# State copies for two units at once, weight sums rounded two slots later, and a reordered start in a scan and feed-forward kernel

## The chip, the cores and the metric

The kernel runs on one core of a Trainium2 chip. The metric is the device time of one execution in microseconds (us). The engines are TensorE (PE, with its weight loads shown as PEld), VectorE (DVE), ScalarE (ACT), GpSimd (POOL) and SyncE (SP), which issues nearly all transfers. Each engine works through its own queue in the order of the program and waits where an operand is not there yet.

## The reference

A chunked linear attention, followed by a two-layer feed-forward block over all its tokens:

```python
# x (4, 8, 768, 32), a (4, 8, 768), B and C (4, 8, 768, 16), chunks of 32
cum = np.cumsum(log_a_of_chunk, axis=-1)
M = einsum(Cc, Bc) * exp(cum_i - cum_j) * causal
y = M @ xc + (Cc @ state) * exp(cum)
state = exp(sum(la)) * state + sum_j(Bc_j * xc_j * exp(cum_last - cum_j))
...
h = y_tokens @ w_in                 # 3072 x 256 by 256 x 2048
out = np.maximum(0.01 * h, h) @ w_out   # 2048 x 256
```

## The kernel before

All engines' queues are written out by hand: an instruction stands in its engine's queue where the Python code issues it, and the framework only adds the waits.

**The scan.** The sequence is cut into 8 chunks of 96 steps, times 4 batches: 32 units `u`, unit `u` being batch `b = u % 4` of chunk `c = u // 4`. A unit covers all 8 heads. For each unit the loop issues `scores(u + 1)` (products of C and B on PE, L387, multiplied by the decay matrix `lt` on DVE, L394), `outputs(u)` (products with the inputs and the state, L405, then copies out of PSUM by ACT), `states(u)` inside it (products for the next chunk's state, L436), and `decay(u + 3)` (a product of `dl` and `dr`, L365, with an exponential on ACT, L358, which gives `lt`). The states leave PSUM by one ACT copy into `stage` (L442), and four POOL copies (L447), one for each of four heads' places, put them into rows 96 to 111 of the next chunk's input tile `xss[c + 1]`, where the unit four later reads them. `state_decay(c + 1)`, once a chunk behind the unit with `b == 1`, multiplies the next B tile `bn` by its decays on POOL (L375); PE's state products of the next chunk need it. Loads for the chunk after the next are issued by SP at `b == 2` and `b == 3`, the `bn` tile last.

**The start.** Units 0 and 1 get their decays by another way (`decay_direct`, L351, from `reach` tiles made on POOL); `fill_less` on DVE and one copy on ACT fill rows of `dr` for the later units; L472 and L473 make `erev`, the decays for `bn`. `keep_warm` (L202) multiplies zeros so that PE has something to do. The surplus load: `fetch_w(0)` is called twice, and the first tile it loads is never read.

**The weights** come as 64-bit numbers and are decoded on the way: five passes for each of 16 blocks `f`, on DVE with help by ACT. From unit 10 on one pass follows each unit (`decode(1)`), 22 in all; in the feed-forward part three passes follow each group.

**The feed-forward part.** Matrices are split into a high and a low part, a product is three PE instructions (L556). The first two token blocks are done for 16 weight blocks in 32 groups: six products of the first layer into one of four PSUM banks, `activate` on ACT (L542, L543), the low half on DVE (L547), which frees the bank, and from the fifth group on six products of the second layer. The other four token blocks use fused products (`strassen`), which need sums of weight blocks (`sh`, `sl`) and of tokens (`token_forms`, which start in `decoded()` when all passes are done). A weight sum is five or four operations on POOL (L129, L139), a rounding to `sh` on ACT (L148, in `sums_high`) and the rest `sl` on POOL (L149). For the first two pairs of blocks, decoded during the scan, the sums are rebuilt ahead of the feed-forward loop (`rebuilt_sums`).

Of the kernel before, what the change touches and what calls it, by code (L numbers as in the profile page):

```python
# [47 lines left out]
def scan_ffn(ctx: ExitStack, tc: tile.TileContext, a_l, bc_l, c_l, bn_l, x_l, w_l, out_l):  # L48
# [75 lines left out]
        add_weights(q, w32s[f - 1][:, :2 * 128], w32s[f][:, :2 * 128])  # L124

    def rebuilt_sums(q):
        a = spare[2].rearrange("p (n c) -> p n c", n=2)
        f = slice(2 * q, 2 * q + 2)
        nc.gpsimd.tensor_tensor(  # L129
            out=a, in0=wh[:, f, :2 * 128], in1=wl[:, f, :2 * 128], op=ALU.add  # L130
        )
        add_weights(q, a[:, 0], a[:, 1])
        settle(2 * q + 1)

    def add_weights(q, a1, a2):
        s = s32s[q] = spare[q % 2].rearrange("p (n c) -> p n c", n=4)

        def tt(out, in0, in1, op):
            nc.gpsimd.tensor_tensor(out=out, in0=in0, in1=in1, op=op)  # L139

        tt(s[:, 0], a2[:, :128], a2[:, 128:], ALU.add)
        tt(s[:, 1], s[:, 0], a1[:, :128], ALU.subtract)
        tt(s[:, 2], a1[:, :128], a2[:, :128], ALU.subtract)
        tt(s[:, 3], a1[:, 128:], s[:, 1], ALU.subtract)
        defer(sums_high, 2 * q + 1)

    def sums_high(f):
        nc.scalar.copy(sh[:, f // 2], s32s[f // 2])  # L148
# [1 line left out]
            out=sl[:, f // 2], in0=s32s[f // 2], in1=sh[:, f // 2], op=ALU.subtract  # L150
        )

    spare, owed = None, collections.deque()
    ready = set()

    def decode_rest(f):
# [78 lines left out]
        alloc_x(c)  # L235
    fetch_x(0)
    fetch_bn(0)
    fetch_w(0)

    upto = sc1.tile([Q, QE], F32, name="upto")  # L240
    upto_b = sc1.tile([Q, QE], BF16, name="upto_b")
# [156 lines left out]
    def outputs(u):  # L398
        c, b = divmod(u, NB)
        kk = QE if c else Q  # L400
        mt, xs = lts[u], xss[c][:, b]
        bank = 6 + u % 2
        for h in range(NH):
            g, hh = divmod(h, 4)
            nc.tensor.matmul(  # L405
                ps[hh * D:(hh + 1) * D, bank, g * Q:(g + 1) * Q],
                lhsT=xs[:kk, h * D:(h + 1) * D], rhs=mt[:kk, h, :], start=True, stop=True,
            )
        if u:
            states(u)  # L410
        yp = ps[:, bank, :2 * Q].rearrange("p (g i) -> p g i", g=2)
        i = 0
        while i < Q:
            t, col = divmod(u * Q + i, TS)
            n = min(Q - i, TS - col)
            to, of = slice(col, col + n), slice(i, i + n)
            if t < 2:
                hi = xfa[:, 2 * t:2 * t + 2, 0, to]
                nc.scalar.copy(hi, yp[:, :, of])
                nc.vector.tensor_tensor(  # L420
                    out=xfa[:, 2 * t:2 * t + 2, 1, to], in0=yp[:, :, of], in1=hi, op=ALU.subtract
                )
            else:
                nc.scalar.copy(y[:, t - 2, :, to], yp[:, :, of])
            i += n

    def states(u):
# [4 lines left out]
        if c + 1 < NC:  # L432
            for h in range(NH):
                g, hh = divmod(h, 4)
                n0 = (b * NH + h) * N
                nc.tensor.matmul(  # L436
                    ps[hh * D:(hh + 1) * D, bank, 2 * Q + g * D:2 * Q + (g + 1) * D],
                    lhsT=bns[c][:kk, n0:n0 + 2 * N], rhs=xs[:kk, h * D:(h + 1) * D],
                    start=True, stop=True,
                )  # L440
            stage = pst.tile([128, 2, D], F32, name="stage")
            nc.scalar.copy(  # L442
                stage, ps[:, bank, 2 * Q:2 * Q + 2 * D].rearrange("p (g d) -> p g d", g=2)
            )
            to = xss[c + 1][Q:QE, b].rearrange("n (g h d) -> n g h d", g=2, d=D)
            for hh in range(4):
                nc.gpsimd.tensor_copy(to[:, :, hh], stage[hh * D:hh * D + N])  # L447

    nc.vector.tensor_scalar(
        out=la, in0=la, scalar1=1e-6, scalar2=1.0, op0=ALU.max, op1=ALU.min,  # L450
# [5 lines left out]
    nc.scalar.activation(la[:, DIRECT * NH:], la[:, DIRECT * NH:], AF.Ln)  # L456
    nc.vector.tensor_copy(after_r, after)
    nc.vector.tensor_copy(dl[:Q], upto_b.unsqueeze(1).to_broadcast([Q, SLOTS, QE]))
    nc.scalar.copy(
        dr[Q:Q + 3 * NH, 0], less[Q:Q + 3 * NH].unsqueeze(2).to_broadcast([3 * NH, NH, Q])  # L460
    )
    for u in range(DIRECT):
        fill_reach(u)
    decay_mask(DEC)
    decay_mask(6)
    split_sums(0, 0, nc.scalar)
    fill_less(1)
    decay_direct(0, DEC)
    decay_exp(0, DEC)
    scores(0)  # L470
    fill_less(2)
    nc.tensor.matmul(ps[:QE, DEC, :ncols], lhsT=after, rhs=la, start=True, stop=True)  # L472
    nc.scalar.activation(erev, ps[:QE, DEC, :ncols], AF.Exp)  # L473
    decay_direct(1, 6)
    fetch_rows(DIRECT, 4)
    decay_exp(1, 6)
    state_decay(0)
    fetch_bc(1)
    fetch_x(1)
# [4 lines left out]
    for u in range(NU):  # L484
# [1 line left out]
        if u + 1 < NU:  # L486
            scores(u + 1)
        outputs(u)
        if u == 1:
            states(0)  # L490
        if u == 0:
            keep_warm(DEC, 4)
            decay(2)
# [10 lines left out]
        if u == 4:  # L504
            split_sums(1, 7)
        if u == 0:
            fill_less(3)
        if 1 <= u <= 4:
            fill_later(u + 3, u + 4)
# [14 lines left out]
    tmp = late.tile([128, 6, TS], F32, name="tmp")  # L524
    ob = late.tile([128, 4, TS], F32, name="ob")
    c1, u2, u3 = (tmp[:, i] for i in range(3))
    spare = [tmp[:, i] for i in range(3)]

    jobs = collections.deque()

# [76 lines left out]


    def decoded():
        settle()  # L610
        dec.close()
        xfb = ctx.enter_context(
            tc.tile_pool(name="xfb", bufs=1, side="right", reuse_waits="tile")
# [4 lines left out]
        for js in token_forms(1):  # L618
            jobs.extend(js)

    for q in owed:
        rebuilt_sums(q)
    behind = 4
    for q in range(NP):
        for e in range(2):
            f = 2 * q + e
            assert f in ready
            for t in range(2):
                bank = 2 * e + t
                for k in range(2):  # L630
                    x = xfa[:, 2 * t + k]
                    product(ps[:, bank], layer_one(f, k), (x[:, 0], x[:, 1]), k == 0, k == 1)
                low = activate(bank, f, t)
                if passes:
                    decode(3)
                    settle()
                    if not passes:
                        decoded()
                low()
                work(2)  # L640
                if q or len(todo) > behind:
# [104 lines left out]
```

## Time and profile before

| | before |
|---|---|
| median of 3 runs | 348.39 us (347.0 to 351.26) |
| the profiled execution, its own time | 344.38 us |
| its span in the profile | 342.7 us |
| mean granted PE clock | 0.97 |
| scan, from the start to the first product of the feed-forward part | 79.25 us |
| feed-forward part, to the end | 263.4 us |

A row of a timeline reads: start, duration, engine, line, operation, out<-in, count, and in brackets the idle time of the engine before it with what ended it. Rows that are merged show the whole stretch with its count. In a window of time the columns are the busy time of PE, PEld, DVE, ACT and POOL with the instructions in brackets, then the granted clock, the share of DMA time and GB/s. In a group the columns are count, busy time, mean ns of one, and the idle time before it. PE rows that overlap are pipelined; their ends are modelled.

### The profile page before, as it was taken

How to read it: one execution, taken by the hardware profiler on the slowest of the kernel's cores; microseconds unless marked ns; L12 is line 12 of the kernel's file. 1: busy time of each engine (PE TensorE's matmuls, PEld its weight loads, DVE VectorE, ACT ScalarE, POOL GpSimd, SP SyncE). 2: the span in 40 equal slices, each digit the busy share in tenths (PEclk: the TensorE clock that was granted, in tenths of full speed). 3: DMA queues.
4: the chain of work that ended last, by engine and by line, in shares of the span. 5: the costliest groups of instructions: out<-in, count | busy, mean ns of one | idle time of the engine just before them, and what ended most of it. 6: DMA issues, size and time to landing. Idle time of an engine off the chain costs nothing.

```text
span 342.7 us, 6283 instructions
## 1 busy us (share of the span) xinstructions
PE 320.9 (94%) x2406; PEld 249.8 (73%) x2407; DVE 214.3 (63%) x367; ACT 187.4 (55%) x369; POOL 116.7 (34%) x202
## 2 busy tenths in 40 slices
PE   6899979799499999999999989999999999999995
PEld 3465646456388888888888868888888888888884
DVE  7398858575599999332376536665547666545661
ACT  4356848561776776565365446554466455445451
POOL 8175688888454454884000053000040000000000
PEclk9699989879899999999999999999999999999999
DMA  7745963903033330000002000000003000000003
GB/s 222 206 147 135 260 192 114 264 5 122 2 130 122 118 124 0 0 2 0 0 28 98 0 0 2 0 0 0 2 0 122 2 0 2 2 0 0 0 2 122
DMA packets 10273, 21.83 MB, mean 64 GB/s; under 512 B 2723, under 2 KB 4611, under 8 KB 10243
## 3 DMA queue, kind: packets, MB, share of 16 engines
q1 hardware_dynamic: 10099, 21.35, 20.1%
q8 instruction: 19, 0.31, 0.4%
q14 instruction: 11, 0.09, 0.1%
q10 hardware_dynamic: 144, 0.07, 0.1%
HBM read 18.13 MB, written 3.29 MB: 63 GB/s over the span
## 4 chain that ended last, share of the span: by engine, by line
PE 74%; issue 12%; POOL 10%; ACT 2%; DVE 2%; POOLq 0%; ACTq 0%; DVEq 0%
PE ps L556 61%; PE ps L387 4%; POOL xs L447 4%; PE ps L365 3%; PE ps L405 3%; POOL tmp L139 1%; POOL bn L375 1%; PE ps L436 1%; POOL tmp L129 1%; ACT lt L358 1%; DVE lt L394 1%; POOL xfa L296 1%; PE ps L202 1%; PE ps L351 1%; POOL xfa L591 0%
## 5 line engine op out<-in xcount | busy, mean ns | idle before, releaser
L556 PE MATMUL ps<-gs,wh 128*128 128x512 f32 x384 | 135.8, 389 | 0.0
L542 ACT ACTIVATE gs<-ps 128x512 fp32r<-128x512 f32 x96 | 57.4, 598 | 68.5 <-DVE ps L658 36.6
L547 DVE TENSOR_TENSOR gs<-ps,gs 128x512 fp32r<-128x512 f32 x96 | 65.8, 685 | 31.1 <-ACT ps L543 31.0
L556 PEld LDWEIGHTS ps<-gs,wh 128*128 128x128 f32 x384 | 72.2, 188 | 15.1
L556 PE MATMUL ps<-gs,wl 128*128 128x512 f32 x192 | 74.7, 389 | 0.0
L556 PE MATMUL ps<-xfa,wh 128*128 128x512 f32 x160 | 57.7, 397 | 5.7 <-DVE gs L547 5.7
L543 ACT ACTIVATE ps<-ps 128x512 f32<-128x512 f32 x96 | 56.9, 593 | 0.0
L658 DVE TENSOR_TENSOR tmp<-ps,tmp 128x512 f32<-128x512 f32 x32 | 22.1, 691 | 54.5 <-PE ps L556 49.3
L394 DVE TENSOR_TENSOR lt<-ps,lt 112x384 f32<-112x384 f32 x64 | 32.7, 552 | 19.0 <-PE ps L387 17.7
L447 POOL COPY xs<-stage 16x64 f32<-16x64 f32 x112 | 38.4, 343 | 16.6 <-ACT stage L442 10.8
L556 PEld LDWEIGHTS ps<-gs,wl 128*128 128x128 f32 x192 | 36.1, 188 | 7.5
L556 PEld LDWEIGHTS ps<-xfa,wh 128*128 128x128 f32 x160 | 30.6, 191 | 12.6 <-DVE gs L547 6.2
L556 PE MATMUL ps<-xfb,sh 128*128 128x512 f32 x96 | 36.0, 389 | 0.0
L658 DVE TENSOR_TENSOR ps<-ps,tmp 128x512 f32<-128x512 f32 x48 | 33.6, 699 | 2.5
L556 PE MATMUL ps<-xfa,wl 128*128 128x512 f32 x80 | 31.6, 395 | 0.0
L358 ACT ACTIVATE lt<-ps 112x768 f32<-112x768 f32 x32 | 26.0, 812 | 7.8 <-PE ps L351 3.5
L556 PE MATMUL ps<-xfb,wh 128*128 128x512 f32 x64 | 25.0, 391 | 1.5 <-ACT tmp L661 1.5
L387 PE MATMUL ps<-bc 32*112 32x192 f32 x256 | 24.8, 407 | 1.4 <-DVE lt L394 1.3
L387 PEld LDWEIGHTS ps<-bc 32*112 32x112 f32 x256 | 12.8, 189 | 12.3 <-DVE lt L394 6.8
L591 POOL TENSOR_TENSOR xfb<-tmp,xfb 128x512 fp32r<-128x512 f32 x6 | 7.7, 1293 | 40.2 <-ACT xfb L595 40.2
L556 PEld LDWEIGHTS ps<-xfb,sh 128*128 128x128 f32 x96 | 18.0, 188 | 3.8
L661 ACT COPY tmp<-ps 128x512 f32<-128x512 f32 x16 | 9.4, 587 | 18.4 <-PE ps L556 18.4
(93 smaller groups left out, 390.0 us busy)
## 6 DMA issues: line engine op xcount, KB each, us to landing
raw<-w_l SPq DMA_DIRECT2D x17, 512.0 KB, 4.2
xs<-x_l SPq DMA_DIRECT2D x8, 384.0 KB, 4.7
out_l<-ob SPq DMA_DIRECT2D x12, 256.0 KB, 2.1
bn<-bn_l SPq DMA_DIRECT2D x8, 231.0 KB, 6.2
bc<-bc_l SPq DMA_DIRECT2D x6, 224.0 KB, 3.6
bc<-bc_l SPq DMA_DIRECT2D x2, 608.0 KB
bc<-c_l SPq DMA_DIRECT2D x12, 96.0 KB, 3.2
dr<-parts_d SPq DMA_DIRECT2D x11, 9.0 KB
```

What stands on the lines that cost most here:

```text
L358: nc.scalar.activation(lt.rearrange("p (g h) i -> p g (h i)", g=2), ps[:QE, bank:bank + 2, :4 * Q], AF.Exp)
L365: nc.tensor.matmul(ps[:QE, DEC + g, :4 * Q].rearrange("p (h i) -> p h i", i=Q), lhsT=dl[:KD, b], rhs=dr[:KD, b, 4 * g:4 * g + 4], start=Tr ...
L387: nc.tensor.matmul(ps[:QE, r, :2 * Q].rearrange("p (h i) -> p h i", h=2), lhsT=bc[rows, b * QE:(b + 1) * QE], rhs=spread[rows, :, b], star ...
L394: nc.vector.tensor_tensor(out=lt[:, g], in0=ps[:QE, g, :2 * Q], in1=lt[:, g], op=ALU.mult)
L405: nc.tensor.matmul(ps[hh * D:(hh + 1) * D, bank, g * Q:(g + 1) * Q], lhsT=xs[:kk, h * D:(h + 1) * D], rhs=mt[:kk, h, :], start=True, stop= ...
L447: nc.gpsimd.tensor_copy(to[:, :, hh], stage[hh * D:hh * D + N])
L542: nc.scalar.activation(g[:, 0], hp, AF.Prelu, alpha=0.01)
L543: nc.scalar.activation(hp, hp, AF.Prelu, alpha=0.01)
L547: nc.vector.tensor_tensor(out=g[:, 1], in0=hp, in1=g[:, 0], op=ALU.subtract)
L556: nc.tensor.matmul(out, lhsT=w[a], rhs=x[b], start=start and i == 0, stop=stop and i == 2, skip_group_check=more,)
L658: nc.vector.tensor_tensor(out=out, in0=ps[:, bank], in1=u, op=ALU.add)
L661: nc.scalar.copy(c1, ps[:, 0])
```

## The change

Four edits. The state copies: `states` of an even unit only issues its products; that of the odd unit copies both units' states with one ACT copy and four POOL copies of twice the size. The surplus load goes. The weight sums: `sums_high` is put on a list and runs two groups later; the two rebuilt sums are issued in the loop, with scratch tiles of their own, and `decoded()` waits for the list to be empty. The start: the row fills for slot 1 move to ACT, those for slot 2 behind unit 0; two warming products are added; unit 1's decay products come ahead of L472.

```diff
     def rebuilt_sums(q):
-        a = spare[2].rearrange("p (n c) -> p n c", n=2)
+        a = spare[4 + q % 2].rearrange("p (n c) -> p n c", n=2)
...
-        settle(2 * q + 1)
     def add_weights(q, a1, a2):
-        s = s32s[q] = spare[q % 2].rearrange("p (n c) -> p n c", n=4)
+        s = s32s[q] = spare[q % 4].rearrange("p (n c) -> p n c", n=4)
...
-        defer(sums_high, 2 * q + 1)
+        delayed.append([2, sums_high, 2 * q + 1])
...
+    def late_sums():
+        for d in list(delayed):
+            d[0] -= 1
+            if d[0] < 0:
+                delayed.remove(d)
+                d[1](d[2])
...
     fetch_bn(0)
-    fetch_w(0)
...
+        if u == 1:
+            states(0)
         if u:
             states(u)
...
-            stage = pst.tile([128, 2, D], F32, name="stage")
+            if b % 2 == 0:
+                return
+            stage = pst.tile([128, 2, 2, D], F32, name="stage")
             nc.scalar.copy(
-                stage, ps[:, bank, 2 * Q:2 * Q + 2 * D].rearrange("p (g d) -> p g d", g=2)
+                stage, ps[:, 6:8, 2 * Q:2 * Q + 2 * D].rearrange("p b (g d) -> p b g d", g=2)
             )
-            to = xss[c + 1][Q:QE, b].rearrange("n (g h d) -> n g h d", g=2, d=D)
+            to = xss[c + 1][Q:QE, b - 1:b + 1].rearrange("n b (g h d) -> n b g h d", g=2, d=D)
             for hh in range(4):
-                nc.gpsimd.tensor_copy(to[:, :, hh], stage[hh * D:hh * D + N])
+                nc.gpsimd.tensor_copy(to[:, :, :, hh], stage[hh * D:hh * D + N])
...
-    fill_less(1)
+    keep_warm(1, 2)
     decay_direct(0, DEC)
     decay_exp(0, DEC)
     scores(0)
-    fill_less(2)
-    nc.tensor.matmul(ps[:QE, DEC, :ncols], lhsT=after, rhs=la, start=True, stop=True)
-    nc.scalar.activation(erev, ps[:QE, DEC, :ncols], AF.Exp)
     decay_direct(1, 6)
     fetch_rows(DIRECT, 4)
     decay_exp(1, 6)
+    nc.tensor.matmul(ps[:QE, DEC, :ncols], lhsT=after, rhs=la, start=True, stop=True)
+    nc.scalar.activation(erev, ps[:QE, DEC, :ncols], AF.Exp)
...
-    for q in owed:
-        rebuilt_sums(q)
...
                 low = activate(bank, f, t)
+                if t == 0 and owed:
+                    rebuilt_sums(owed.popleft())
                 if passes:
                     decode(3)
                     settle()
-                    if not passes:
-                        decoded()
+                late_sums()
+                if not (passes or delayed or owed or forms):
+                    decoded()
                 low()
```

On POOL, at the end of the scan and the beginning of the feed-forward part, the rows were (a row stands for as many equal instructions as its last figure says; `w_...` are decoded weight tiles, `tmp` is the scratch):

```order
L375 TENSOR_TENSOR bn<-bn,erev 112x512
L447 COPY xs<-stage 16x2x32 x16
L375 TENSOR_TENSOR bn<-bn,erev 112x512
L447 COPY xs<-stage 16x2x32 x8
L129 TENSOR_TENSOR tmp<-wh,wl 128x512
L139 TENSOR_TENSOR tmp<-tmp 128x128 x4
L149 TENSOR_TENSOR sl<-tmp,sh 128x512
L129 TENSOR_TENSOR tmp<-wh,wl 128x512
L139 TENSOR_TENSOR tmp<-tmp 128x128 x4
L149 TENSOR_TENSOR sl<-tmp,sh 128x512
L139 TENSOR_TENSOR tmp<-w_1375 128x128
```

and are now (line numbers are those of the changed kernel, some 10 higher):

```order
L381 TENSOR_TENSOR bn<-bn,erev 112x512
L457 COPY xs<-stage 16x4x32 x8
L381 TENSOR_TENSOR bn<-bn,erev 112x512
L457 COPY xs<-stage 16x4x32 x4
L129 TENSOR_TENSOR tmp<-wh,wl 128x512
L138 TENSOR_TENSOR tmp<-tmp 128x128 x4
L129 TENSOR_TENSOR tmp<-wh,wl 128x512
L138 TENSOR_TENSOR tmp<-tmp 128x128 x4
L138 TENSOR_TENSOR tmp<-w_1282 128x128
```

Half as many copies, each of two units, stand between two decays of `bn`, and the subtractions for `sl` no longer stand behind their own sums: all sums of the first two pairs come first.

On ACT, at the same place, ahead of and behind the first activation (`gs<-ps`), before:

```order
L117 CAST wh<-w_1092 128x512
L424 COPY y<-ps 128x2x96 x3
L148 CAST sh<-tmp 128x512 x2
L542 ACTIVATE gs<-ps 128x512
L543 ACTIVATE ps<-ps 128x512
L80 ACTIVATE w_1375<-raw 128x512
```

and now:

```order
L117 CAST wh<-w_1020 128x512
L432 COPY y<-ps 128x2x96 x3
L551 ACTIVATE gs<-ps 128x512
L552 ACTIVATE ps<-ps 128x512
L80 ACTIVATE w_1282<-raw 128x512
L117 CAST wh<-w_1187 128x512
L551 ACTIVATE gs<-ps 128x512
L552 ACTIVATE ps<-ps 128x512
L80 ACTIVATE w_1298<-raw 128x512
L551 ACTIVATE gs<-ps 128x512
L552 ACTIVATE ps<-ps 128x512
L117 CAST wh<-w_1282 128x512
```

The two roundings `sh<-tmp` are gone from ahead of the first activation. The first of them now stands right behind these rows, behind the third group's activations, and the other behind the fifth's.

On PE, at the start, from the sums of the decays (L314) to the scores of unit 1, before:

```order
L314 MATMUL ps<-upto,la 128x96
L351 MATMUL ps<-xfa,after_r 112x384 x4
L387 MATMUL ps<-bc_102 112x192 x4
L472 MATMUL ps<-la,after 112x256
L351 MATMUL ps<-xfa,after_r 112x384 x4
L202 LDWEIGHTS idle
L202 MATMUL ps<-idle 128x512
L387 MATMUL ps<-bc_102 112x192 x4
```

and now:

```order
L320 MATMUL ps<-upto,la 128x96
L209 LDWEIGHTS idle
L209 MATMUL ps<-idle 128x512
L209 LDWEIGHTS idle
L209 MATMUL ps<-idle 128x512
L357 MATMUL ps<-xfa,after_r 112x384 x4
L393 MATMUL ps<-bc_102 112x192 x4
L357 MATMUL ps<-xfa,after_r 112x384 x4
L485 MATMUL ps<-la,after 112x256
L209 LDWEIGHTS idle
L209 MATMUL ps<-idle 128x512
L393 MATMUL ps<-bc_102 112x192 x4
```

Two warming products are new ahead of unit 0's decay products, and the product for `erev` has moved behind those of unit 1.

More of the change, by code (lines that the diff above doesn't have):

```diff
@@ L151, in sums_high @@
         )
-    spare, owed = None, collections.deque()
+    spare, owed, delayed = None, collections.deque(), []
+    def late_sums():
[4 more added lines that the diff above has]
+                d[1](d[2])
     ready = set()
@@ L458, in scan_ffn @@
     nc.vector.tensor_copy(dl[:Q], upto_b.unsqueeze(1).to_broadcast([Q, SLOTS, QE]))
-    nc.scalar.copy(
-        dr[Q:Q + 3 * NH, 0], less[Q:Q + 3 * NH].unsqueeze(2).to_broadcast([3 * NH, NH, Q])
-    )
+    for b in range(2):
+        nc.scalar.copy(
+            dr[Q:Q + 3 * NH, b], less[Q:Q + 3 * NH].unsqueeze(2).to_broadcast([3 * NH, NH, Q])
+        )
     for u in range(DIRECT):
@@ L488, in scan_ffn @@
         outputs(u)
-        if u == 1:
-            states(0)
         if u == 0:
@@ L506, in scan_ffn @@
         if u == 0:
+            fill_less(2)
             fill_less(3)
@@ L526, in scan_ffn @@
     c1, u2, u3 = (tmp[:, i] for i in range(3))
-    spare = [tmp[:, i] for i in range(3)]
+    spare = [tmp[:, i] for i in range(6)]
     jobs = collections.deque()
@@ L609, in decoded @@
     def decoded():
-        settle()
+        while delayed:
+            late_sums()
         dec.close()
@@ L636, in scan_ffn @@
                     settle()
-                    if not passes:
-                        decoded()
+                late_sums()
+                if not (passes or delayed or owed or forms):
+                    decoded()
                 low()
```

## The prediction

> **What bounds the kernel now.** I read the page first: busy shares, slices, and the shares of the chain that ended last.
>
> ```profile
> PE 320.9 (94%) x2406; PEld 249.8 (73%) x2407; DVE 214.3 (63%) x367; ACT 187.4 (55%) x369; POOL 116.7 (34%) x202
> POOL 8175688888454454884000053000040000000000
> PEclk9699989879899999999999999999999999999999
> PE 74%; issue 12%; POOL 10%; ACT 2%; DVE 2%; POOLq 0%; ACTq 0%; DVEq 0%
> ```
>
> TensorE (PE) holds the chain, but GpSimd (POOL) has a tenth of it, all in the first ten slices: the scan and its end. After about 94 us PE runs without a gap, and nothing of the change lies there on the path. So I looked for PE's gaps up to 94 us, in the timeline.
>
> ```profile
> 39.00 8.17 POOL L447 COPY xs<-stage 16x64 f32<-16x64 f32 x16
> 47.24 1.05 POOL L375 TENSOR_TENSOR bn<-bn,erev 112x512 f32<-112x512 f32 x1
> 45.34 0.54 PE L405 MATMUL ps<-lt,xs 112*32 112x96 f32 x16
> 48.35 0.33 PE L436 MATMUL ps<-xs,bn 112*32 112x32 f32 x16 [2.48 <-POOL bn L375]
> 65.80 0.33 PE L436 MATMUL ps<-xs,bn 112*32 112x32 f32 x16 [2.39 <-POOL bn L375]
> 78.14 1.17 PE L405 MATMUL ps<-lt,xs 112*32 112x96 f32 x32
> 79.25 0.50 PE L556 MATMUL ps<-xfa,wh 128*128 128x512 f32 x1
> ```
>
> POOL works in order. Sixteen state copies (L447) took 8.17 us, the decay of the next B chunk (L375) stood behind them, and PE waited 2.48 us for it at unit 16 and 2.39 us at unit 24. The row at 78.14 holds the output products of units 30 and 31, that at 79.25 the first product of the feed-forward part. Each gap is followed by a stretch at half the granted clock (last figures of a window: clock, DMA share, GB/s):
>
> ```profile
> 50.00:52.00 2.00, 2.00 (x39) 1.38 (x42) 1.62 (x3) 0.55 (x4) 1.77 (x5) 0.50 0.15 41
> 66.00:68.00 2.00, 2.00 (x38) 1.01 (x29) 0.17 (x1) 1.24 (x3) 1.59 (x8) 0.57 0.63 220
> 70.00:72.00 2.00, 2.00 (x42) 1.21 (x34) 1.42 (x3) 0.82 (x4) 1.75 (x5) 0.50 0.00 0
> ```
>
> What a unit takes without and with that clock stands in the chain, at the output products (L405) of units 19, 21, 25 and 27:
>
> ```profile
> 54.52 0.47 PE ps L405 x16
> 57.86 0.47 PE ps L405 x16
> 67.72 0.80 PE ps L405 x16
> 73.23 0.47 PE ps L405 x16
> ```
>
> Two units in 3.34 us, 1.67 each, against 5.51 us, 2.76 each. The last gap is at the end of the scan:
>
> ```profile
> 84.59 0.39 PE L556 MATMUL ps<-xfa,wh 128*128 128x512 f32 x1
> 87.43 0.62 ACT L148 CAST sh<-tmp 128x512 fp32r<-128x512 f32 x1 [4.52 <-POOL tmp L139]
> 90.71 0.80 PE L556 MATMUL ps<-xfa,wh 128*128 128x512 f32 x1 [5.73 <-DVE gs L547]
> 92.00:94.00 2.00, 2.00 (x7) 1.52 (x7) 1.97 (x5) 1.23 (x4) 0.53 (x1) 0.61 0.04 8
> 90.71 73.03 PE ps L556 x315
> 202.61 136.31 PE ps L556 x600
> ```
>
> ScalarE (ACT) works in order too: the rounding of two weight sums (L148) stands ahead of the first activation and waits 4.52 us for POOL's sums, so no PSUM bank comes free and PE stops for 5.73 us. Its first products afterwards run at 0.61 of the clock: 315 products took 73.03 us, 0.2318 each, and later 600 took 136.31, 0.2272 each; the difference is 315 x 0.0046 = 1.4 us.
>
> **The change, part by part.**
>
> *Weight sums rounded later.* The two roundings, each with a subtraction on POOL behind it, leave the head of ACT's queue and stand two slots back; the first activation follows PE at once. The sums on POOL stay where they are, and nobody needs them before the products of the form groups, after 168 us (below). That removes 5.73 us and the 1.4 us of slow clock: **7.1 us**. What is late next: VectorE (DVE), whose low halves free the banks.
>
> ```profile
> 96.00:100.00 4.00, 4.00 (x19) 3.32 (x18) 3.93 (x7) 3.93 (x8) 1.69 (x1) 1.00 0.43 144
> ```
>
> DVE (third busy figure) is full at 3.93 of 4.00 us while PE is full too. Before, PE's stall gave DVE no lead: it waited for ACT itself. Now PE needs bank 0 again only after four groups of six products (79.25 to 84.98), and DVE needs by then two decode passes and one low half, some 3 us. I cost this at nothing, with 0 to 3 us as bounds: at most the lead of one group is lost. The token forms wait for the last sum, which now comes two slots later, 2 x 12 x 0.2272 = 5.5 us:
>
> ```profile
> 159.23 1.29 POOL L591 TENSOR_TENSOR tmp<-y 128x512 f32<-128x512 f32 x1
> 168.32 0.39 PE L556 MATMUL ps<-xfb,wh 128*128 128x512 f32 x1
> ```
>
> Their last work on POOL ends at 160.5 and PE's first use of them is at 168.3; of these 7.8 us 2.3 are left, so that costs nothing either.
>
> *State copies for two units.* 56 copies of 16x128 replace 112 of 16x64, and 14 copies by ACT replace 28.
>
> ```profile
> L447 POOL COPY xs<-stage 16x64 f32<-16x64 f32 x112 | 38.4, 343 | 16.6 <-ACT stage L442 10.8
> L447 POOL COPY xs<-stage x3: 232/233/1233, 61.6 to 63.2; 16x64 f32<-16x64 f32 x3
> 136.65 0.46 POOL L139 TENSOR_TENSOR tmp<-tmp,w 128x128 f32<-128x128 f32 x1
> 139.13 1.30 POOL L149 TENSOR_TENSOR sl<-tmp,sh 128x512 fp32r<-128x512 f32 x1 [0.73 <-ACT sh L148]
> ```
>
> A copy takes 0.233 us undisturbed. No row shows one of 128 elements with this pattern: below, 0.233 (size is free); above, 0.466 (all of it scales). POOL's own slope from the last two rows, (1.30 - 0.46)/384 = 2.2 ns an element, gives 0.233 + 0.14 = 0.37, which I take. The mean of 343 ns holds 112 x 0.110 = 12.3 us of disturbance; undisturbed and disturbed copies differ by up to 1 us, and the disturbed ones stand in the stretch with the 22 decode passes on DVE (units 10 to 31), 0.56 us a pass. So POOL needs for four units, with 0.06 us between instructions: before 16 x 0.29 + 1.1 + 4 x 0.56 = 8.0 us as a mean (9.3 us from 39.00 to 48.29, by the rows above), after 8 x 0.43 + 1.1 + 2.2 = 6.8 us, against PE's 4 x 1.67 = 6.7. POOL just keeps up, since a pass that finds POOL idle costs nothing.
>
> The Trainium skill, "SBUF — State Buffer", Who interferes with whom, says that a VectorE operation with two SBUF inputs and a GpSimd one that reads SBUF exclude each other, so that the later one waits for the whole of the other. By it the disturbance goes with DVE's passes and not with the number of copies, as I have counted it; were it shared out per copy, POOL would come to 8 x 0.54 + 1.1 = 5.4 us and have a fifth to spare.
>
> What is late next is the load of that B chunk:
>
> ```profile
> 33.41 0.36 SPq L225 DMA_DIRECT2D bn<-bn_l  x1
> 37.78 1.15 POOL L375 TENSOR_TENSOR bn<-bn,erev 112x512 f32<-112x512 f32 x1 [2.57 <-ACT y L424]
> 39.66 0.35 SPq L225 DMA_DIRECT2D bn<-bn_l  x1
> 58.03 0.37 SPq L225 DMA_DIRECT2D bn<-bn_l  x1
> ```
>
> ACT's copy named at 37.78 was long done; the load issued at 33.41 landed then, 4.4 us later. By that the loads for units 16 and 24 land at 44.1 and 62.4, the decay is done at 45.3 and 63.6, and PE wants it at about 45.7 and 63.3: no wait, or 0.3 us. The pair's copies come one unit later than the even unit's did, but are read three units (5 us) after the stage is filled, and take 1.7 us. The stage copy now spans both banks, so the output products of the next even unit also wait for it on ACT; PE's decay and score products lie between, and I cost that at nothing.
>
> So I take PE's pace of 1.67 to 1.7 us through units 16 to 31. Unit 16 starts at 45.34 and the feed-forward part at 79.25, 33.9 us; at pace it is 14 x 1.7 + 1.1 (from unit 30 on, 78.14 to 79.25) = 24.9. The gain is **9.0 us**: 4.9 of gaps, the rest slow clock and the restarts behind it.
>
> *First two units and the surplus load.*
>
> ```profile
> 7.98 0.98 PE L472 MATMUL ps<-la,after 96*112 96x256 f32 x2 [0.38 <-ACT lt L358]
> 10.04 0.65 PE L202 MATMUL ps<-idle 128*128 128x512 bf16 x1
> 10.62 1.00 PE L387 MATMUL ps<-bc 32*112 32x192 f32 x8
> 16.19 0.59 PE L387 MATMUL ps<-bc 32*112 32x192 f32 x8
> 8.00:10.00 2.00, 2.00 (x6) 1.47 (x6) 1.34 (x3) 0.39 (x1) 0.70 (x2) 0.56 0.29 101
> ```
>
> With unit 1's decay products ahead of L472, PE need not wait 0.38 us, but L472's reader on ACT and the warming product behind it now come last, so the scores of unit 1 start at about 10.8 instead of 10.62: -0.2 us. The two warming products fill PE's idle time before 5.6 us. If they keep the clock (0.56 from 8 us on), the scores take 0.59 as at 16.19 and not 1.00, and everything to 15.8 us shrinks alike: +2.0. I take 0, nearer the row at 10.04, where another warming product did not lift the clock. The fills move into DVE's idle time and ACT's; the missing 512 KB leave the queues early, where PE waits for no load. Only one load leaves the load queue's order, none changes its place, so this costs nothing.
>
> Sum: 7.1 + 9.0 + 0 = 16.1 us. The profiled execution took 344.4 us, a span of 342.7; less 16.1 it is 328.3. The runs have a median of 348.4, 4 us above it, which I keep: **332**.
>
> **Rivals.**
>
> *The scan stays held up.* POOL at 6.8 of 6.7 us has no room; if copies cost 0.466 and loads land 2 us later, POOL needs 7.5 a four-unit round and a gap of 1 to 2 us comes back with its slow clock. For it: DMA shares near 1 from 60 to 66 us. Against it: the passes met copies that queued, and will meet fewer. Half of the 9.0 is lost: 337. Chance 0.20.
>
> *DVE becomes the bound behind the scan.* It loses up to 3 us of the 7.1: 335. Chance 0.08.
>
> *The slow clock is not the gaps' doing.* If as many units run at half clock anyway (17, 25 and 26, at 1.1 us each) and the first products too (1.4), 4.7 us come back: 337. All three slow stretches lie right behind a gap, which speaks against it. Chance 0.06. The Trainium skill, "TensorE: Matmul & The Clock Gate", Why this matters for your kernels, lets the clock drop only for idle gaps above some 3 us; by that the gaps of 2.4 us would be harmless, and here the trace differs.
>
> *Slower: the wide copy falls out of its pace.* Three strides a side on 16 partitions may cost far more than its elements. The scan breaks even where 8(c + 0.06) + 3.3 = 9.3, at c = 0.69 us; the 7.1 us at the end are eaten, over five to six rounds, at c = 0.85. At 1.2 us a round takes 13.4 us, 4.1 more than before, in six rounds 25 us: 348 + 25 - 7 = 366. Nothing in the trace shows such a copy. Chance 0.04. *The roundings still end up ahead of an activation* that PE waits for: 339, chance 0.02.
>
> **How the numbers follow.** My forecast has 0.60: 332, from 326 (clock kept at the start, the 4 us between runs and profile halved) to 335. The others lie at 335 to 339, but for the slow case. The range of 325 to 339 leaves out some 0.15. Two per cent, about what a measurement of this kernel can tell from no change, is below 341.4 or above 355.4: faster 0.91, same 0.05, slower 0.04.
>
> **What would show it.** Right: no PE wait of 2 us for `bn` or copies before the feed-forward part, which starts near 70 us; clock 1.0 from 46 us on; copies of about 0.37 us undisturbed; the first activation on ACT within 2 us of PE's first products, and no PE gap behind them. Wrong: copies above 0.7 us, a wait for the B load, or DVE named as PE's releaser between 70 and 100 us.

## The result, and the profile after

The changed kernel has a median of 330.64 us (328.58 to 343.9, 4 runs) against 347.69 us of the kernel before (346.69 to 351.26, 4 runs): a ratio of 0.947, 95% interval 0.937 to 0.957. The profiled execution took 329.74 us, a span of 327.6, that is 15.1 us less than the span of before. In a later series of runs the same kernel gave 335.26 us (329.23 to 336.84, 6 runs) against 348.79: a ratio of 0.951, 0.943 to 0.959. Ratios here leave out executions over 1.5% above the fastest of their kernel; the medians hold all of them.

The page after, lines of parts 1, 2 and 4 (busy shares, slices, shares of the chain):

```profile
PE 315.7 (96%) x2409; PEld 246.4 (75%) x2409; DVE 217.8 (66%) x366; ACT 185.9 (57%) x356; POOL 103.3 (32%) x146
POOL 8143677797535446960000423000130000000000
PEclk9997999999999999999999999999999999999999
PE 69%; issue 14%; DVE 7%; DMA 3%; POOL 3%; ACT 2%; POOLq 0%; SPq 0%; DVEq 0%; ACTq 0%
```

POOL's share of the chain falls from 10% to 3%. In its place stand DVE (7%, before 2%) and transfers (3%, before none). The clock has one low slice left, the fourth. POOL's timeline between two B chunks, and its copies as the view of one source line and the view of groups have them:

```profile
42.76 1.06 POOL L381 TENSOR_TENSOR bn<-bn,erev 112x512 f32<-112x512 f32 x1 [0.55 <-PE ps L393]
43.88 2.29 POOL L457 COPY xs<-stage 16x128 f32<-16x128 f32 x4
46.75 2.41 POOL L457 COPY xs<-stage 16x128 f32<-16x128 f32 x4 [0.58 <-ACT stage L452]
50.16 1.51 POOL L381 TENSOR_TENSOR bn<-bn,erev 112x512 f32<-112x512 f32 x1 [1.00 <-DMA bn<-bn_l]
58.15 1.06 POOL L381 TENSOR_TENSOR bn<-bn,erev 112x512 f32<-112x512 f32 x1 [1.30 <-DMA bn<-bn_l]
```

```profile
L457 POOL COPY xs<-stage x56: 284/291/1233, 15.7 to 67.5; 16x128 f32<-16x128 f32 x56
```

```profile
L457 POOL COPY xs<-stage 16x128 f32<-16x128 f32 x56 | 24.4, 436 | 20.1 <-ACT stage L452 17.4
```

A wide copy takes 0.291 us where nothing disturbs it (the median of the second fence). The copies of four units are done in two runs of 2.3 to 2.4 us instead of one of 8.17, POOL waits for work in between, and in front of the decay it now waits for the load. PE's timeline shows what is left of its two gaps, the end of the scan, and the beginning of the feed-forward part:

```profile
43.87 0.54 PE L411 MATMUL ps<-lt,xs 112*32 112x96 f32 x16
59.26 0.33 PE L444 MATMUL ps<-xs,bn 112*32 112x32 f32 x16 [0.65 <-POOL bn L381]
69.93 0.50 PE L565 MATMUL ps<-xfa,wh 128*128 128x512 f32 x1
84.01 0.50 PE L565 MATMUL ps<-xfa,wh 128*128 128x512 f32 x1 [0.18 <-DVE gs L556]
90.13 0.50 PE L565 MATMUL ps<-xfa,wh 128*128 128x512 f32 x1 [0.39 <-DVE gs L556]
```

Unit 16 starts at 43.87, the feed-forward part at 69.93. In three stages the 15.1 us are: 1.5 up to unit 16 (45.34 before), 7.85 from there to the first feed-forward product (26.06 against 33.91), 5.75 behind it (257.7 against 263.4).

### The profile page after: what moved, and what is told of

The parts are those of the page before. It is cut to its first block, busy times and chain, and to the rows that moved or that the text cites. A ratio compares the mean times of both kernels' runs of the same rounds, so it can differ in the third digit from the quotient of the medians.

```text
span 327.6 us, 6208 instructions
## 1 busy us (share of the span) xinstructions
PE 315.7 (96%) x2409; PEld 246.4 (75%) x2409; DVE 217.8 (66%) x366; ACT 185.9 (57%) x356; POOL 103.3 (32%) x146
## 4 chain that ended last, share of the span: by engine, by line
PE 69%; issue 14%; DVE 7%; DMA 3%; POOL 3%; ACT 2%; POOLq 0%; SPq 0%; DVEq 0%; ACTq 0%
PE ps L565 60%; DMA bn<-bn_l 3%; PE ps L393 3%; PE ps L411 2%; PE ps L371 2%; DVE lt L400 2%; DVE w L98 1%; DVE gs L556 1%; ACT lt L364 1%; DVE w L106 1%; PE ps L444 1%; POOL xfa L302 1%; POOL bn L381 1%; DVE wl L165 1%; PE ps L357 1%
## 5 line engine op out<-in xcount | busy, mean ns | idle before, releaser
L565 PE MATMUL ps<-xfa,wh 128*128 128x512 f32 x160 | 57.0, 393 | 0.6 <-DVE gs L556 0.6
L457 POOL COPY xs<-stage 16x128 f32<-16x128 f32 x56 | 24.4, 436 | 20.1 <-ACT stage L452 17.4
L393 PE MATMUL ps<-bc 32*112 32x192 f32 x256 | 23.1, 373 | 1.4 <-DVE lt L400 0.9
L393 PEld LDWEIGHTS ps<-bc 32*112 32x112 f32 x256 | 12.3, 173 | 12.4 <-DVE lt L400 9.2
L117 ACT CAST wh<-w 128x512 fp32r<-128x512 f32 x16 | 9.9, 619 | 17.4 <-DVE w L106 17.4
```

The costliest lines, as they stand in the source:

```text
L117: nc.scalar.copy(wh[:, f], w32s[f])
L393: nc.tensor.matmul(ps[:QE, r, :2 * Q].rearrange("p (h i) -> p h i", h=2), lhsT=bc[rows, b * QE:(b + 1) * QE], rhs=spread[rows, :, b], star ...
L457: nc.gpsimd.tensor_copy(to[:, :, :, hh], stage[hh * D:hh * D + N])
L565: nc.tensor.matmul(out, lhsT=w[a], rhs=x[b], start=start and i == 0, stop=stop and i == 2, skip_group_check=more,)
```

## The experiments

Four kernels do one edit each on the kernel before, four alter the changed kernel, and four more, run together on one chip, take up what the first eight had left open. This table has what their timelines show, in us: the start of the output products of units 1, 8 and 16, the stage from unit 16 to the first feed-forward product, and from there to the end.

| kernel | unit 1 | unit 8 | unit 16 | 16 to FF | FF to end |
|---|---|---|---|---|---|
| before | 16.72 | 31.42 | 45.34 | 33.9 | 263.4 |
| load_only | 16.52 | 31.22 | 45.14 | 34.7 | 263.9 |
| start_only | 14.44 | 31.54 | 45.64 | 33.7 | 263.2 |
| pairs_only | 16.47 | 33.25 | 47.26 | 28.3 | 264.6 |
| sums_only | 15.81 | 33.92 | 49.77 | 33.0 | 258.2 |
| changed | 14.44 | 30.10 | 43.87 | 26.1 | 257.7 |
| after_again | 18.58 | 35.51 | 49.67 | 27.4 | 257.7 |
| no_warming | 18.59 | 38.66 | 53.09 | 26.8 | 257.8 |
| no_warming_again | 18.58 | 35.09 | 48.80 | 27.2 | 257.4 |
| narrow_copies | 18.58 | 35.45 | 49.15 | 35.7 | 258.2 |
| light_decode | 14.43 | 28.80 | 42.69 | 33.9 | 256.2 |
| bn_first | 14.37 | 31.36 | 45.14 | 26.4 | 257.7 |
| deep_loads | 18.58 | 35.38 | 50.11 | 26.9 | 257.8 |
| deep_light | 14.43 | 28.73 | 46.20 | 26.4 | 256.6 |

**The four edits, each alone on the kernel before.**

*The state copies alone.*

```diff
+        if u == 1:
+            states(0)
...
+            if b % 2 == 0:
+                return
+            stage = pst.tile([128, 2, 2, D], F32, name="stage")
...
+                nc.gpsimd.tensor_copy(to[:, :, :, hh], stage[hh * D:hh * D + N])
```

> The kernel before with the state copies for two units as its only edit. Theory (POOL's queue of copies made the two gaps at units 16 and 24 and the slow clock behind them): the feed-forward part starts at 71 to 72 us instead of 79.3, no PE wait above 1 us for bn, its length stays at 263 us; span 334 to 336. Rival (the gaps belong to the loads of bn, the copies only stood in the same queue): the waits of 2.4 us stay, the feed-forward part starts at 78 to 79 us and the span is 341 to 343.

Measured: 338.68 us (336.7 to 342.06, 4 runs), ratio 0.974, 0.965 to 0.984. PE's gaps, and POOL's decay ahead of the first, in their timelines:

```profile
62.06 1.42 POOL L375 TENSOR_TENSOR bn<-bn,erev 112x512 f32<-112x512 f32 x1 [2.06 <-ACT wh L117]
63.54 0.33 PE L438 MATMUL ps<-xs,bn 112*32 112x32 f32 x16 [1.78 <-POOL bn L375]
87.00 0.80 PE L558 MATMUL ps<-xfa,wh 128*128 128x512 f32 x1 [5.72 <-DVE gs L549]
```

One of the two gaps of the scan is left, and the stage from unit 16 takes 28.3 us; the gap behind the scan stands as before, 5.72 us against 5.73. The two gains are separate. The gap that is left is not one of copies: POOL stood idle for 2.06 us ahead of that decay, and by the trace's semaphores the load of its B chunk landed at 61.90 us, just before it (the ACT instruction that the row names is not what the decay waits for). So the rival has a part of it: the first feed-forward product was expected at 71 to 72 us and came at 75.52, 1.9 us of it because unit 16 already started later, behind a stretch at half clock from 27.3 to 34.1 us.

*The roundings alone.*

```diff
-        defer(sums_high, 2 * q + 1)
+        delayed.append([2, sums_high, 2 * q + 1])
...
+                late_sums()
```

> The kernel before with the weight sums' rounding two slots later as its only edit. Theory (ACT's order made the gap of 5.7 us at the end of the scan): the scan ends at 79 us as before, PE's gap behind it is under 1.5 us in all, the feed-forward part takes 257 to 259 us instead of 263.4; span 336 to 338. Rival (DVE has no room for it and takes the gain back): PE waits 4 us or more for DVE's low halves in the first ten groups, the part takes 262 us or more.

Measured: 342.56 us (341.61 to 343.73, 4 runs), ratio 0.988, 0.982 to 0.994. The feed-forward part takes 258.2 us, 5.2 less than before, and its longest wait in the timeline behind the scan is now one for DVE:

```profile
97.44 0.50 PE L563 MATMUL ps<-xfa,wh 128*128 128x512 f32 x1 [0.62 <-DVE gs L554]
```

The gap of 5.73 us is gone. This execution's scan ran at half speed from 22 to 39.5 us and from 60 to 73.5, so it ended at 82.80 us and not at 79 as expected, which takes back a part of the gain.

*The start alone.*

```diff
-    fill_less(1)
+    keep_warm(1, 2)
...
-    fill_less(2)
-    nc.tensor.matmul(ps[:QE, DEC, :ncols], lhsT=after, rhs=la, start=True, stop=True)
-    nc.scalar.activation(erev, ps[:QE, DEC, :ncols], AF.Exp)
     decay_direct(1, 6)
     fetch_rows(DIRECT, 4)
     decay_exp(1, 6)
+    nc.tensor.matmul(ps[:QE, DEC, :ncols], lhsT=after, rhs=la, start=True, stop=True)
+    nc.scalar.activation(erev, ps[:QE, DEC, :ncols], AF.Exp)
```

> The kernel before with only the start reordered (row fills, two warming products, unit 1's decay products ahead of those for the B decays); the surplus load stays. Theory (the warming products keep PE's clock through 8 to 15 us): clock 1.0 from 8 to 15 us, output products of unit 1 near 14.5 us instead of 16.7. What is left at the end of the scan: 0 to 2.3 us; if the loads and POOL set the pace of units 8 to 31, nothing. Span 340 to 343. Rival (the clock falls anyway, the gain in the changed kernel came from the missing load): clock 0.5 from 8 to 15 us and unit 1 at 16.5 to 17 us.

Measured: 344.24 us (343.74 to 351.87, 10 runs), ratio 0.992, 0.989 to 0.996. Unit 1 comes 2.28 us earlier, and at unit 8 nothing is left of it (31.54 against 31.42): there was a stretch at half clock from 25.7 to 32.5 us, and behind it POOL is as late as before:

```profile
56.09 0.33 PE L436 MATMUL ps<-xs,bn 112*32 112x32 f32 x16 [2.35 <-POOL bn L375]
76.65 0.36 PE L405 MATMUL ps<-lt,xs 112*32 112x96 f32 x2 [1.82 <-POOL xs L447]
```

That is one execution, with a span of 342.5 us against 342.7. Over all its runs this edit is worth more: the ratio comes to some 2.6 us, and its interval to 1.3 to 4.0.

*The load alone.*

```diff
     fetch_bn(0)
-    fetch_w(0)
```

> The kernel before without the surplus load as its only edit. Theory (PE waits for no load at the start): unit 1's output products at 16.7 us as before, clock 0.5 from 8 to 15 us, span 342 to 343.5. Rival (512 KB less in the queues let the decay rows come 2 us sooner, and PE with them): unit 1 at 14.5 to 15.5 us, span 340 to 341.

Measured: 347.57 us (344.97 to 351.79, 10 runs), ratio 0.999, 0.995 to 1.003: no difference. The product of the four ratios is 0.954, that of all edits 0.947 and 0.951.

**The changed kernel, altered.**

*Narrow copies.* ACT still copies two units at once, POOL's copies are 112 of 16x64 again.

```diff
-                nc.gpsimd.tensor_copy(to[:, :, :, hh], stage[hh * D:hh * D + N])
+            for k in range(2):
+                for hh in range(4):
+                    nc.gpsimd.tensor_copy(to[:, k, :, hh], stage[hh * D:hh * D + N, k])
```

> The changed kernel with one ACT copy for two units as it is, but eight POOL copies of 16x64 behind it instead of four of 16x128: the number of POOL copies as before, issued in pairs of units. Theory (the number of copies counts: 0.233 + 0.06 us each, against 0.288 + 0.06 for the wide ones): POOL needs 16 x 0.29 + 1.1 + 1.5 to 2.2 = 7.3 to 8 us for four units of 6.7 us, falls behind, and gaps of 1 to 3 us for bn or copies come back: feed-forward part from 73 to 77 us. Rival (the pairing, that is the later issue and fewer ACT copies, is what helped): it starts at 70 to 71 us.

Measured: 338.27 us (337.9 to 344.81, 5 runs), ratio 0.973, 0.966 to 0.979. The profiled execution took 344.81 us, the other four 337.9 to 338.8. POOL's and PE's timelines:

```profile
42.16 7.40 POOL L458 COPY xs<-stage 16x64 f32<-16x64 f32 x16
49.64 2.05 POOL L381 TENSOR_TENSOR bn<-bn,erev 112x512 f32<-112x512 f32 x1
```

```profile
51.74 0.44 PE L444 MATMUL ps<-xs,bn 112*32 112x32 f32 x16 [2.06 <-POOL bn L381]
70.10 0.33 PE L444 MATMUL ps<-xs,bn 112*32 112x32 f32 x16 [2.09 <-POOL bn L381]
82.20 0.35 PE L411 MATMUL ps<-lt,xs 112*32 112x96 f32 x2 [1.83 <-POOL xs L458]
```

Both gaps are back, at the same units and nearly of the same size as before (2.48 and 2.39), a third has joined them, and the stage from unit 16 takes 35.7 us. The feed-forward part starts at 84.87 us, later than the 73 to 77 expected: unit 16 itself is 5 us later than in the changed kernel, because of a slow start (below). In all five executions the mean granted clock is 0.978 to 0.985, in nine of the changed kernel's ten 0.989 to 1.00, so the slow stretches are not those of one execution. What brings the gain is the number of POOL's copies, not their pairing or the fewer copies on ACT.

*Lighter decoding behind the scan.* Two passes instead of three in each slot of the first pair of weight blocks.

```diff
-                    decode(3)
+                    decode(3 if q else 2)
```

> The changed kernel with two decode passes instead of three behind each of the first four groups of the feed-forward part; the passes left out there come later, nothing is left out in all. Theory (DVE is late for PE's banks between 80 and 92 us by 1.3 us, as POOL's subtractions hold its passes): with 2.8 us less of DVE work in those groups PE's waits there go, and the part takes 256.2 to 256.8 us instead of 257.7. Rival (PE's loss there is not DVE's): 257.7 as before, or more since the passes that come later meet the same wait.

Measured: 334.66 us (331.75 to 335.09, 4 runs), ratio 0.961, 0.954 to 0.968. From the first feed-forward product to the end it takes 256.2 us, 1.5 less than the changed kernel, with PE busy without a gap, as windows behind the scan show:

```profile
82.00:86.00 4.00, 4.00 (x19) 3.34 (x18) 4.00 (x7) 2.90 (x6) 3.10 (x5) 1.00 0.02 5
86.00:90.00 4.00, 4.00 (x19) 3.30 (x19) 4.00 (x6) 3.33 (x7) 3.77 (x5) 1.00 0.37 133
```

In the changed kernel PE (the first busy figure) is held there, while DVE (the third) is full in both:

```profile
80.00:84.00 4.00, 3.83 (x17) 2.82 (x16) 3.96 (x6) 1.91 (x5) 2.80 (x3) 1.00 0.28 110
88.00:92.00 4.00, 3.61 (x16) 2.69 (x15) 4.00 (x6) 2.83 (x6) 3.10 (x5) 1.00 0.38 130
```

That accounts for the 1.35 us by which the roundings gained less than forecast: with three passes a slot DVE is late by so much behind the scan. But the scan, which has the same code as the changed kernel's, took 6.7 us longer in this execution. PE's and POOL's timelines:

```profile
43.77 1.58 POOL L381 TENSOR_TENSOR bn<-bn,erev 112x512 f32<-112x512 f32 x1 [2.79 <-DMA bn<-bn_l]
45.41 0.33 PE L444 MATMUL ps<-xs,bn 112*32 112x32 f32 x16 [2.02 <-DMA bc<-c_l]
63.56 1.05 POOL L381 TENSOR_TENSOR bn<-bn,erev 112x512 f32<-112x512 f32 x1 [3.59 <-DMA bn<-bn_l]
64.67 0.33 PE L444 MATMUL ps<-xs,bn 112*32 112x32 f32 x16 [2.94 <-POOL bn L381]
```

Half clock followed each of PE's waits (45.9 to 52.7 us, 66.4 to 69.8). PE's first wait is named after a load of C rows, but it ended with POOL's decay, at 45.4 us; POOL stood idle ahead of both decays, for 2.79 and 3.59 us, until the B chunk had landed. With the copies off the path, it was the loads that held the scan in this execution.

*B chunk ahead of the inputs.* `fetch_x(c + 2)` is issued one unit later, behind `fetch_bn(c + 2)`, which so moves up in the queue of loads.

```diff
             fetch_bc(c + 2)
-            fetch_x(c + 2)
         if b == 3 and c + 2 < NC:
             fetch_bn(c + 2)
+            fetch_x(c + 2)
```

> The changed kernel with the load of bn issued ahead of the load of x at the third unit of a chunk instead of x first at the second. Theory (POOL's waits of 1.0 to 1.3 us for bn, and PE's of 0.2 and 0.65 behind them, come from 384 KB that go ahead): bn lands about 1 us sooner against PE's work, the waits fall under 0.3 us, feed-forward part from 69 us instead of 69.9. Rival (the queue order on SP, not the bytes, delays it; or x becomes late): bn as late as before, or output products waiting for x, 70 us or more.

Measured: 333.27 us (331.06 to 335.55, 4 runs), ratio 0.959, 0.951 to 0.967. POOL's waits, from the view of waits (us in total, times, longest), up to 72 us:

```profile
POOL xs L457 <- ACT stage L452: 20.3, 10, 4.6
POOL bn L381 <- ACT erev L486: 1.9, 1, 1.9
```

No wait for the load of a B chunk is left (3.5 us in the changed kernel), and PE has no wait for `bn`. Yet the stage from unit 16 takes 26.4 us, not less than 26.1, and the feed-forward part starts at 71.56 us, not at 69. So no gain is seen from taking away the remaining 0.2 and 0.65 us of PE's waits; one of that size could hide, since this stage took 26.1 and 27.4 us in two executions of the changed kernel.

*No warming products.*

```diff
-    keep_warm(1, 2)
```

> The changed kernel without the two new warming products at the start. Theory (they bring PE to full speed before unit 0's decay products, the reordering alone does not): the four decay products of unit 0 take 1.8 us from 5.6 us on as in the runs without them, unit 1's output products start at 15.8 to 16.8 us instead of 14.4, the feed-forward part 0 to 2 us later than 69.9. Rival (the order of unit 1's decay products made the gain): unit 1 at 14.4 to 15 us without them too. The granted clock of the records says nothing before its first change; the products' durations decide.

Measured: 337.64 us (332.81 to 339.73, 4 runs), ratio 0.962, 0.952 to 0.972. The profiled execution took 339.73 us; of the 10 us by which its span is longer than the changed kernel's, 9.2 are lost up to unit 16 (53.09 us). Unit 1 starts at 18.59 us, later than either side had expected. PE's timeline, scores of units 6 and 10, and windows (columns as before; the clock is the third figure from the end):

```profile
29.29 1.00 PE L393 MATMUL ps<-bc 32*112 32x192 f32 x8
40.49 0.62 PE L393 MATMUL ps<-bc 32*112 32x192 f32 x8
```

```profile
28.00:30.00 2.00, 2.00 (x25) 1.41 (x16) 1.10 (x5) 1.13 (x2) 0.00 (x0) 1.00 0.71 215
```

Scores take 1.00 us until 39 us, where they take 0.59 to 0.62 at full speed, while the granted clock reads 1.00 throughout. The half speed is read from the products' durations; the first change that the trace records, to full clock, comes at 40.6 us. PE is busy without a gap in this window (2.00 of 2.00 us).

**Four more, on one chip: chance or cause?** The profile of narrow_copies has warming products and half speed up to 28 us. Either the half speed at the start comes by chance, or something in that kernel brought it.

*The changed kernel again, unaltered.*

> The changed kernel itself, unaltered, beside the three runs below on one chip. Theory (executions of one and the same scan differ by when its loads land: the first feed-forward product came at 69.93 us in the changed kernel's profile and at 76.61 in that of light_decode, whose scan is the same code): single runs between 328 and 336 us, a median of 331 to 334, and a first feed-forward product anywhere from 69 to 77 us. Rival (light_decode itself made the scan slower): runs within 2 us of 330, first feed-forward product at 69.5 to 70.5.

Measured: 335.26 us (329.23 to 336.84, 6 runs), a little above the 331 to 334 expected. PE's timeline of the profiled execution, scores of units 5 and 6:

```profile
26.14 1.00 PE L393 MATMUL ps<-bc 32*112 32x192 f32 x8
28.75 0.59 PE L393 MATMUL ps<-bc 32*112 32x192 f32 x8
...
66.38 0.33 PE L444 MATMUL ps<-xs,bn 112*32 112x32 f32 x16 [1.92 <-POOL bn L381]
```

The same code ran at half speed to 28 us here and at full speed from 5.6 us in its first profile. That moves unit 16 by 5.8 us (49.67 against 43.87); the wait of 1.92 us for a B chunk adds to it, and the feed-forward part agrees to 0.1 us. So it was the start, more than the loads that the expectation named, which set these two executions apart. The kernel's ten executions in the two series fall into 328.6 to 331.6 us (five) and 335.0 to 343.9 (five); the two that have a profile lie one in each, and whether the start parts the other eight too isn't shown.

*No warming products, again.* The edit is as above.

> The changed kernel without the two warming products, again. Theory A (the products lift the clock early, worth 1.5 us at unit 16): 1 to 3 us above after_again, products at full speed from some 13 us. Theory B (without them half speed can last far into the scan, as in the profile of no_warming, where the scores still took 1.00 us at 29 us): 5 to 8 us above after_again. If the half speed comes by chance in both kernels, as narrow_copies with its warming products and half speed to 27.5 us suggests, the two medians agree within 1 us.

Measured: 335.59 us (331.48 to 337.55, 6 runs), against 335.26 with them, the last of the three cases. So the warming products don't decide it by themselves. Among the profiles of kernels with the reordered start and the warming products, five have full speed from some 5 us and three half speed to 28; without them both have half speed, to 27 and 41 us. That is too few to say whether they help. Of the kernels with the old start, load_only, pairs_only and sums_only reached full speed at 12 to 14 us; before had it from 4.8 to 8.2 us already, and again from 15.1.

*Loads a chunk earlier.* Three buffers for B chunks and C rows, so that no load waits for a buffer.

```diff
-    pbc = scan.enter_context(tc.tile_pool(name="pbc", bufs=2))
+    pbc = scan.enter_context(tc.tile_pool(name="pbc", bufs=3))
...
+            fetch_bn(c + 2)
+            fetch_c(c + 2)
             alloc_x(c + 2)
+            fetch_x(c + 2)
             fetch_bc(c + 2)
-            fetch_x(c + 2)
-        if b == 3 and c + 2 < NC:
-            fetch_bn(c + 2)
```

> The changed kernel with three buffers instead of two for the scan's C rows and B chunks, whose loads are issued a chunk earlier and never wait for a buffer; the room comes from laying arrays of the first units into y. Theory (what is left to lose in the scan is loads that land after they are wanted: 0.2 and 0.65 us in the changed kernel's profile, 2.0 and 2.9 in light_decode's): no wait of PE for bn or bc above 0.3 us, first feed-forward product at 67 to 70 us, median 1 to 4 us below after_again, single runs closer together. Rival (the queues are full from 30 to 66 us, at DMA shares of 0.7 to 1.1, so the wait only moves to another load): no gain, and the waits stand at xs or at the rows dr and dl.

Measured: 334.57 us (331.04 to 340.63, 6 runs), ratio 0.960, 0.953 to 0.966: no gain over the changed kernel beside it. PE's timeline:

```profile
40.65 0.59 PE L403 MATMUL ps<-bc,bc 32*112 32x192 f32 x8 [0.88 <-DMA dl<-parts_d]
56.24 0.59 PE L403 MATMUL ps<-bc,bc 32*112 32x192 f32 x8 [1.67 <-DMA bc<-bc_l]
```

The rival holds: no wait for a B chunk is left, but the waits moved to the rows `dl` and to `bc<-bc_l`, which now stood last in the order. The stage from unit 16 is 26.9 us. This execution, too, had the slow start, so the feed-forward part began at 76.96 us.

*Both, loads earlier and lighter decoding.*

> deep_loads and two decode passes instead of three a slot in the first group of four activations. The first profile of light_decode had 256.2 us from the first feed-forward product to the end, against 257.7 in the changed kernel. Theory (the two add up): 1.5 us below deep_loads, 256.2 us from the first feed-forward product to the end. Rival (the passes left over hold the bank-freeing low halves later): same as deep_loads or above.

Measured: 331.51 us (328.78 to 337.66, 6 runs), ratio 0.953, 0.948 to 0.959. The feed-forward part takes 256.6 us, 1.2 less than in deep_loads, near the 1.5 of light_decode. The median is 3.1 us under deep_loads and 3.7 under the changed kernel on this chip, but the ratio is within the interval of the changed kernel's, and the start in its profile was the full-speed one: that it beats the changed kernel isn't shown.

## Why the prediction was right

The time forecast was 332 us; measured were 330.64 and 335.26. The sum was 16.1 us and the two spans differ by 15.1, but this agreement holds for an execution with the fast start (full speed from some 5 us) only.

*State copies, 9.0 us: 7.85 measured.* The mechanism was right: no 8 us of copies ahead of a decay, and PE's pace is (26.06 - 1.1)/14, 1.78 us a unit, against 1.7 taken. The copy's price was too high, 0.37 us against 0.291, so a doubled copy costs only 0.06 us more than one of 0.232. The disturbance was 56 x (0.436 - 0.291) = 8.1 us, against 12.3 with twice as many copies: it did not stay with the passes (which would have kept 12.3), nor did it quite halve with the copies (6.2). So the counting by passes, which the prediction drew from the Trainium skill's "SBUF — State Buffer", Who interferes with whom, does not hold as it stands, and the traces lie nearer the copies: over all profiles it is 10.5 to 16.2 us with 112 copies and 5.5 to 9.3 with 56. That the two engines hold each other up is seen: each of the 13 copies of the changed kernel that took over 0.1 us more than the median lies beside a decode pass on DVE. With the lower price and the smaller disturbance POOL has room that the sum didn't give it. The step "no wait, or 0.3 us" for the load that is late next was near for this profile (POOL waits 1.00 and 1.30, PE 0.65 at most) and too narrow for other executions of the same scan: 1.9, 2.0 and 2.9 us. The loads behind those two waits of POOL took 5.2 and 5.8 us from issue to landing, against the 4.4 taken (issued at 44.80 and 52.16 us, landed at 50.00 and 57.99).

*Late roundings, 7.1 us: 5.75 measured.* The gap and the slow clock behind it went as said, the first activation starts 1.7 us behind PE's first product (71.63 against 69.93), and of DVE's bounds of 0 to 3 us, taken as nothing, about 1.4 are real (light_decode: 256.2). "At most the lead of one group is lost" was right; the value of 0 was not. A part of it may come from a side that the prediction had not counted, DVE's own passes held up by POOL's subtractions for `sl`; no run takes these away alone:

```profile
81.08 1.73 POOL L148 TENSOR_TENSOR sl<-tmp,sh 128x512 fp32r<-128x512 f32 x1
85.60 2.99 POOL L148 TENSOR_TENSOR sl<-tmp,sh 128x512 fp32r<-128x512 f32 x2 [2.80 <-ACT sh L147]
```

```profile
77.87 0.68 DVE L106 SCALAR_TENSOR_TENSOR w<-raw,w 128x512 uint32<-128x512 uint32 x1
81.69 1.66 DVE L106 SCALAR_TENSOR_TENSOR w<-raw,w 128x512 uint32<-128x512 uint32 x1
85.87 1.58 DVE L98 SCALAR_TENSOR_TENSOR w<-raw,w 128x512 uint32<-128x512 uint32 x1
87.48 1.66 DVE L106 SCALAR_TENSOR_TENSOR w<-raw,w 128x512 uint32<-128x512 uint32 x1
```

A pass of 0.68 us takes 1.6 beside such a subtraction, three times up to 90 us.

*Start, 0 us, bounds -0.2 to +2.0: the step that failed.* It isn't one number. With the fast start it gains 2.3 us at unit 1 and 1.5 at unit 16; with the slow one it loses 1.9 at unit 1 and 4.3 at unit 16 (49.67 against 45.34). The lower bound of -0.2 is wrong by 4 us, because I took the half speed at the start for something that ends near 15 us in every execution. The upper one of +2.0 is doubtful as well, by the 2.6 us of start_only. That the median over ten executions, between 331.55 and 334.98, falls on the forecast is in part luck: the 4 us added for "the runs against the profile" were meant for something else.

*The surplus load, nothing: right* (0.999).

*Rivals.* "The slow clock is not the gaps' doing" had 0.06 and is half right. In the changed kernel the clock fell behind a wait of 0.64 us only, and did not behind 0.65:

```profile
24.53 1.04 PE L393 MATMUL ps<-bc 32*112 32x192 f32 x8 [0.64 <-DVE lt L400]
```

```profile
26.00:28.00 2.00, 2.00 (x34) 1.01 (x24) 1.03 (x3) 1.11 (x3) 0.30 (x1) 0.50 0.39 145
```

In after_again it didn't fall behind 1.92 us either (the scores behind it take 0.59), in light_decode it did behind 2.02 and 2.94, but not behind the same wait of 0.64 at 24.51. So the reading of before, each gap followed by half clock, was too simple: the length of a gap alone doesn't decide. By the Trainium skill, "TensorE: Matmul & The Clock Gate", Why this matters for your kernels, only gaps of some 3 us would do it; falls behind 0.64 and 2.02 speak against that.

What the traces do show is a grid. The changes of the clock that one execution records lie 3.41 us or a multiple of it apart (in the changed kernel at 5.26, 25.74 and 29.15 us). Counted by such steps, in all fourteen profiles up to 100 us, 19 steps at full clock had PE busy for 2.02 us or less, and the clock fell at the end of 18 of them. Above that it fell in five only, which all began between 18 and 24 us, with 2.63 to 2.79 us busy; what sets these apart is open. The wait of 2.02 us lies in one step, that of 1.92 us in two (windows of light_decode, then of after_again):

```profile
42.47:45.88 3.41, 1.39 (x42) 0.88 (x34) 1.62 (x3) 0.70 (x2) 1.99 (x3) 1.00 0.83 257
```

```profile
62.16:65.58 3.42, 2.30 (x64) 1.37 (x58) 3.15 (x7) 2.67 (x6) 1.09 (x2) 1.00 1.05 251
65.58:68.99 3.41, 2.61 (x66) 1.72 (x68) 1.19 (x3) 1.70 (x5) 2.14 (x6) 1.00 0.97 227
```

So for a gap of some 2 us it counts how much of it falls into one step, and that differs between executions. This is a count over traces; no run moves a gap against the grid on purpose. "The scan stays held up" came true in some executions (light_decode, 76.61 us), by loads and not by POOL's copies. The wide copy was far from the 0.69 us at which the scan would have broken even.

*What would show it:* the feed-forward part near 70 us, the clock at 1.00 from 46 us on, and no gap behind the roundings all came in the first profile; copies at 0.37 did not (0.291). Two signs of being wrong came as well: DVE as PE's releaser between 70 and 100 us, at 84.01 and 90.13, and a wait for the B load, 1.00 and 1.30 us on POOL.

## What to carry to other kernels

When copies on a slow engine stand ahead of work that others wait for, look first at their number: twice the elements cost a quarter more, and narrow_copies shows that the number was what mattered and not the pairing. Work out an edit's effect stage by stage (here to unit 16, to the first product of the next part, to the end): between two executions of the changed kernel the last stage agrees to 0.1 us and the middle one to 1.3, where the sum differs by 7. And before a term at the start is priced, ask whether its state is the same in every execution, and read the speed from the products' durations.

## What the runs showed of the hardware

Until a first change of the clock is recorded, the granted clock reads 1.00 even where products run at half speed: 1.00 us for eight score products at 29.29 in no_warming, 0.59 elsewhere. By the first recorded change, the half speed at the start lasted to some 5, 12 to 14, 27 to 28 or 41 us, and PE being busy without a gap (from 18 us on in after_again and in no_warming) did not end it sooner. What sets the moment is open. One thing goes with it: carried back to the start, the steps of 3.41 us begin 1.0 to 2.4 us behind the span's start in the five profiles with warming products and a fast start, and 0.5 to 0.7 us behind it in the three with a slow one; in the two without warming products, 3.05 and 3.17. Later stretches at half clock lasted 3.4 or 6.8 us in most traces, and 13.7 and 17.1 in sums_only, all multiples of 3.41.

The exclusion of DVE and POOL works in both directions: a copy of 0.291 us took up to 1.233 us, and a DVE pass of 0.68 us 1.66.
